# Attention with two MoE layers on one core: a weight's split parts kept in DRAM, two small scalings made one, and a path for probabilities turned by DMA

## The chip, the cores and the metric

The kernel runs on 1 core of one Trainium2 chip. The metric is the device time of one execution in microseconds (us), the median of several runs; less is better.

## The reference

Attention over 4 batches, 8 heads, 576 positions of 64 features, in which each row keeps its 32 largest scores; its output, as 2304 tokens of 512 features, goes through two feed-forward layers.

```python
scores = (q @ k.T) / 8
kth    = 32nd largest score of the row
scores = where(scores >= kth, scores, -1e9) - max
attn   = exp(scores) / (sum(exp(scores)) + 1e-9)
x = attn @ v                                    # [2304, 512]
x = (1 / (1 + exp(-(x @ w_gate))) * (x @ w_val)) @ w_out    # d_ff 1536
out = max(x @ w_in, 0)**2 @ w_out2                          # d_ff 2048
```

Weights arrive as float64, everything else as float32; the output is float32.

## The kernel before

**Tiles and chunks.** The 2304 tokens are 18 tiles of 128. They are worked through in 11 chunks: chunks 0 to 3 of one tile, chunks 4 to 10 of two. For each chunk all 8 heads go through attention, two heads at a time (class `Pair`, line 199), and then the chunk goes through the two layers. One tile of one head is called a unit here: 128 rows of scores, 144 units in all.

**A unit.** `scores` (line 262) multiplies the turned query by the head's keys on TensorE (PE); keys are split in two parts, kept in DRAM and loaded per head into one of three buffers `kst` (line 236). ScalarE (ACT) copies the scores to `S` (284). `softmax` (287) finds the 32nd largest of each row on VectorE (DVE) with four MAX8 and three MATCH_REPLACE8 passes (294, 300). GpSimd (POOL) makes two numbers a row of it, the mask's and the exponential's bias (304, 305, tile `bs`), ACT and POOL mask the scores (306, 307), ACT takes the exponential and its sum (308), DVE the reciprocal (312, 313), POOL scales the row (322). `transpose` (325) turns the probabilities on PE with matmuls against an identity (340, 358), ACT copies them back (341), and `values` (363) multiplies them by the values in float32 (373). In chunks 0 and 1 the scaling is done by the turning matmul (338).

**Weights.** 64-bit words are loaded 512 KB at a time into `wpool`, a pool of 35 slots, converted to float32, and from chunk 1 on used as two float16 parts: `split` (498) makes the high part on ACT (502) and the low part on DVE (505), every fourth time on POOL (507, 508). Of the 35 slots the split weights hold 34 for good once all are made; eight of these are of `w_out2`, called w2.

**The two layers.** Chunk 0 is computed in plain float32 (`moe32`, 740). The others run `moe` (614): each product is three float16 matmuls. Layer 1 is `l1_pair` (584) and `l1_acc` (620); then comes the turn (lines 660 to 675): ACT squares the result, PE sums columns (`x2pq`, 666), DVE takes the largest (`x2cm`, 668) and the scale `x2s` of it (124 to 129), and ACT and DVE write `x2` in two parts (672, 673). Layer 2 is `l2_pair` (689: `ph`, then `rh`) and `l2_acc` (712), which reads w2 from its eight tiles:

```python
acc2[:, i, 0:DM], gh[:, b_, ...], wblk("w2", a, f, 0, DM),   # lines 717 to 720
```

**Names.** The function begins with `NT, DM = out.shape` (line 87), so that within it, and in all that is defined in it, `DM` is 512.

**What sets the order.** The Tile scheduler orders each engine's instructions by priorities that the code gives: `at(t)` (963) for the weights and chunk 0, `attend` (951) for units, which are asked for a number of units ahead of each step of `moe`. All loads and stores are issued by SyncE (SP), one after the other, in the order that the scheduler sets.

## Time and profile before

| what | value |
|---|---|
| runs | 1314.05, 1313.09, 1314.70 us, median 1314.05 |
| the profiled execution: span from first to last instruction | 1312.3 us |
| what lies around that span, against the median | 1.75 us |
| PE busy | 1214.3 us (93%) |
| DVE busy | 1018.8 us (78%) |
| POOL busy | 838.6 us (64%) |
| ACT busy | 758.5 us (58%) |
| DMA | 113.00 MB, mean 86 GB/s |
| mean granted TensorE clock | 0.969 |

The profiled execution's own time isn't given apart from its span; the median of the runs stands 1.75 us above that span. An engine's busy share is a mean over stages, so the stage decides: the windows view gives busy time of each engine by stretch, the waits view what an engine stood still for, the timeline single instructions with the idle time before them in brackets and what ended it.

### The profile page before, as it was taken

What the parts mean: (1) busy time and instruction counts of PE and PEld (TensorE: products, weight loads), DVE (VectorE), ACT (ScalarE), POOL (GpSimd) and SP (SyncE); (2) the same over time, 40 slices, a digit from 0 to 9 for tenths busy, and PEclk for the clock granted to TensorE, in tenths of its full rate; (3) what the DMA queues carried; (4) which work ended last, traced back from release to release, by engine and by line L of the source; (5) the groups of instructions that cost most, each with busy time, mean ns of one, the idle gap of its engine ahead of it and who ended that gap; (6) DMA issues with size and microseconds to landing.
All of it is one profiled execution on the core that took longest, in us unless ns stands there. A gap on an engine that the chain in (4) does not pass through costs nothing.

```text
span 1312.3 us, 28283 instructions
## 1 busy us (share of the span) xinstructions
PE 1214.3 (93%) x10613; PEld 971.6 (74%) x10613; DVE 1018.8 (78%) x2192; ACT 758.5 (58%) x1500; POOL 838.6 (64%) x1124
## 2 busy tenths in 40 slices
PE   6746798989999899999999999999999999999998
PEld 4535686777978778777888678777876887787775
DVE  6999999999999999989899888985998698210010
ACT  4876767677666665666566655664566566323122
POOL 1988878888676675586567746674576557324223
PEclk9766899999999999999999999999999999999999
DMA  6967861221323221524211233321111110000000
GB/s 187 350 246 252 276 206 56 62 64 54 94 67 103 61 62 28 132 70 137 82 53 36 73 101 96 95 67 53 42 48 42 46 37 10 17 2 1 17 1 16
DMA packets 116328, 113.00 MB, mean 86 GB/s; under 512 B 73440, under 2 KB 87776, under 8 KB 116192
## 3 DMA queue, kind: packets, MB, share of 16 engines
q1 hardware_dynamic: 116192, 111.19, 28.3%
q8 instruction: 84, 1.38, 0.4%
q14 instruction: 52, 0.43, 0.1%
HBM read 96.99 MB, written 14.16 MB: 85 GB/s over the span
## 4 chain that ended last, share of the span: by engine, by line
PE 70%; DVE 14%; POOL 6%; ACT 3%; DMA 3%; issue 3%; SPq 1%; ACTq 0%; POOLq 0%; DVEq 0%
PE acc L717 13%; PE ph L696 12%; PE pg L593 9%; PE pv L593 9%; PE acc L633 9%; PE xp L373 6%; PE sp L281 6%; PE tp L340 4%; DVE mx L294 3%; DVE W L300 3%; POOL W L307 1%; PE qpt L244 1%; DMA wv_r<-in_moe_w_val_dram 1%; DVE wv_c L462 1%; POOL W L322 1%
## 5 line engine op out<-in xcount | busy, mean ns | idle before, releaser
L294 DVE MAX8 mx<-W 128x8 f32<-128x576 f32 x432 | 327.4, 758 | 7.7
L307 POOL TENSOR_TENSOR W<-S,W 128x576 f32<-128x576 f32 x144 | 208.1, 1445 | 32.6 <-ACT W L306 32.1
L696 PE MATMUL ph<-x,wi_w 128*128 128x256 f16 (+1 forms) x1920 | 209.2, 260 | 8.0 <-ACT x L672 7.4
L300 DVE MATCH_REPLACE8 W<-mx,W 128x576 f32<-128x576 f32 x288 | 213.7, 742 | 0.0
L717 PE MATMUL acc<-w_w,rh 128*128 128x512 f16 x816 | 195.8, 379 | 1.5 <-POOL rh L709 1.5
L696 PEld LDWEIGHTS <-wi_w 128*128 128x128 f16 x1920 | 167.2, 99 | 39.7 <-issue 10.4
L306 ACT ACTIVATE W<-S,bs 128x576 f32<-128x576 f32 x144 | 112.0, 778 | 108.2 <-POOL bs L304 107.9
L593 PE MATMUL pg<-xs,wg_w 128*128 128x256 f16 (+1 forms) x1440 | 156.0, 257 | 3.1 <-ACT xs L547 1.6
L308 ACT ACTIVATE W<-W,bs 128x576 f32<-128x576 f32 x144 | 112.0, 778 | 71.8 <-POOL W L307 71.3
L593 PE MATMUL pv<-xs,wv_w 128*128 128x256 f16 (+1 forms) x1440 | 152.7, 257 | 0.2 <-DVE x2cm L668 0.2
L281 PE MATMUL sp<-kst,qt 128*128 128x288 f32 x608 | 130.6, 327 | 9.0 <-ACT S L284 5.0
L593 PEld LDWEIGHTS <-wg_w 128*128 128x128 f16 x1440 | 122.4, 98 | 18.3 <-issue 2.7
L633 PEld LDWEIGHTS <-wo_w 128*128 128x128 f16 x1440 | 123.1, 98 | 16.6 <-issue 3.7
L593 PEld LDWEIGHTS <-wv_w 128*128 128x128 f16 x1440 | 122.7, 98 | 16.4 <-issue 3.3
L717 PEld LDWEIGHTS <-rh 128*128 128x128 f16 x816 | 77.7, 98 | 76.4 <-POOL rh L709 2.0
L605 DVE TENSOR_TENSOR th<-pv,th 128x512 f32<-128x512 f32 (+1 forms) x60 | 36.2, 603 | 119.1 <-PE pv L593 117.9
L633 PE MATMUL acc<-gh,wo_w 128*128 128x256 f16 (+1 forms) x1200 | 124.8, 254 | 2.4 <-POOL gh L609 2.4
L294 DVE MAX8 mx<-S 128x8 f32<-128x576 f32 x144 | 107.4, 746 | 15.7 <-ACT S L284 15.4
L708 POOL TENSOR_TENSOR r<-r 128x512 f32<-128x512 f32 (+1 forms) x80 | 74.7, 936 | 59.8 <-ACT rh L707 58.8
L341 ACT COPY PT<-tp 128x512 f32<-128x512 f32 x144 | 83.7, 581 | 47.6 <-PE tp L340 39.3
L322 POOL TENSOR_SCALAR we<-W,rz 128x64 f32<-128x64 f32 x128 | 41.5, 324 | 108.0 <-DVE rz L313 72.7
L300 DVE MATCH_REPLACE8 W<-mx,S 128x576 f32<-128x576 f32 x144 | 106.8, 742 | 0.3 <-issue 0.3
(297 smaller groups left out, 2224.8 us busy)
## 6 DMA issues: line engine op xcount, KB each, us to landing
kst<-ks SPq DMA_DIRECT2D x104, 288.0 KB, 2.9
v<-in_v_dram SPq DMA_DIRECT2D x112, 128.0 KB, 2.2
qn<-in_q_dram SPq DMA_DIRECT2D x128, 64.0 KB, 2.2
wi_r<-in_moe_w_in_dram SPq DMA_DIRECT2D x16, 512.0 KB, 6.8
w_r<-in_moe_w_out_dram SPq DMA_DIRECT2D x16, 512.0 KB, 4.7
wg_r<-in_moe_w_gate_dram SPq DMA_DIRECT2D x12, 512.0 KB, 8.0
wv_r<-in_moe_w_val_dram SPq DMA_DIRECT2D x12, 512.0 KB, 7.2
wo_r<-in_moe_w_out_dram SPq DMA_DIRECT2D x12, 512.0 KB, 7.0
```

Source lines behind the costliest of these rows:

```text
L281: nc.tensor.matmul(sp[:, e, 0:HALF], l, r, start=(x == 0), stop=(x == len(ops) - 1))
L294: m8 = nc.vector.max(mx[:, r], cur)
L300: nc.vector.match_replace(wk, mx[:, r], cur, NEG)
L306: nc.scalar.activation(wk, ss, AF.Relu, bias=bs[:, 0:1], scale=-BIG)
L307: nc.gpsimd.tensor_tensor(wk, ss, wk, op=ALU.subtract)
L308: nc.scalar.activation(wk, wk, AF.Exp, bias=bs[:, 1:2], scale=SCALE, accum_out=bs[:, 2:3])
L341: nc.scalar.copy(ptr[:, :, i * P : (i + 1) * P], tp.rearrange("p (c t) -> p c t", c=CB))
L373: nc.tensor.matmul(xp[j * D : (j + 1) * D, o : o + n], vj, pj, start=(si == 0 and c == 0), stop=(c == NB - 1), skip_group_check=True,)
L593: nc.tensor.matmul(pp[:, e * N : (e + 1) * N], wblk(wd, a, c, f0, P), xs[:, b_, c, :], start=(e == 0 and n == 0), stop=(n == 3 * KM - 1), ...
L633: nc.tensor.matmul(acc[:, d // 2, (d % 2) * N : (d % 2 + 1) * N], wblk("wo", a, f, d * P, P), gh[:, b_, e * N : (e + 1) * N], start=(f == ...
L696: nc.tensor.matmul(ph[:, e * N : (e + 1) * N], wblk("wi", a, c, f0, P), x2[:, b_, c, :], start=(e == 0 and n == 0), stop=(n == 3 * KM - 1) ...
L717: nc.tensor.matmul(acc2[:, i, 0:DM], gh[:, b_, e * N + i * P : e * N + (i + 1) * P], wblk("w2", a, f, 0, DM), start=(f == 0 and x == 0), s ...
```

## The change

1. **`bs`.** The two POOL operations of a unit on 128x1 (lines 304, 305) become one on 128x2, the first and the last of the row's 32 maxima times a constant tile `bsc` that two DVE memsets fill at the start.
2. **w2.** `split` writes each of w2's eight split tiles (512 KB) to DRAM (`w2s`). `l2_pair` of every chunk from 1 on loads the tile it needs into a slot of `wpool` (`w2t`), and `l2_acc` reads that. So w2 no longer holds eight slots.
3. **A second path for probabilities and values**, for chunk indices of `DM` and more: float16 parts of the scaled probabilities, turned by a DMA, and values in two float16 parts that are prepared once and loaded from DRAM; such units' `tail` comes two units later (`TLAG`) instead of one. The module gets a constant `DM = 4`; line 87, which sets `DM` in the function, stays.
4. `rz` gets a second operation, times 1.0 in chunk indices below `DM`.

The diff, cut to its core:

```diff
+DM = 4
+WE = 3
+TLAG = 2
+PSC = float(2.0**14)
...
+    bsc = const.tile([P, 2], F32, name="bsc")
+    nc.vector.memset(bsc[:, 0:1], -SCALE)
+    nc.vector.memset(bsc[:, 1:2], BIG)
...
+    def prep_values(b, hp):
+        vn = wpool.tile([P, 2 * CB + 1, D], F32, tag="w", name=f"vn_{b}_{hp}")
+        load_v(vn, b, hp)
...
+        d = dpool.tile([P, 2 * (2 * CB + 1) * D], F16, name=f"vs_{b}_{hp}", tag=f"vs_{b}_{hp}")
+        nc.sync.dma_start(d, v16.rearrange("p a c d -> p (a c d)"))
+        vscr[(b, hp)] = d
...
-            nc.gpsimd.tensor_scalar(bs[:, 0:1], mx[:, TOPK // 8 - 1, 7:8], BIG, None, op0=ALU.mult)
-            nc.gpsimd.tensor_scalar(bs[:, 1:2], mx[:, 0, 0:1], -SCALE, None, op0=ALU.mult)
+            nc.gpsimd.tensor_tensor(
+                bs[:, 0:2], mx.rearrange("p a b -> p (a b)")[:, 0 : TOPK : TOPK - 1], bsc, op=ALU.mult
+            )
...
-            nc.vector.tensor_scalar(rz, bs[:, 2:3], 1e-9, None, op0=ALU.add)
+            nc.vector.tensor_scalar(
+                rz, bs[:, 2:3], 1e-9, 1.0 if self.ci < DM else 1.0 / PSC, op0=ALU.add, op1=ALU.mult
+            )
...
-            return wk, ident
+            if self.ci < DM:
+                return wk, ident
+
+            wt = apool.tile([P, 2 * SM + 4 * ST], F16, tag="PT", bufs=2, name=f"w16_{tt}_{h}")
+            w16 = wt[:, 0 : 2 * SM].rearrange("p (a k) -> p a k", a=2)
+            nc.scalar.copy(w16[:, 0], wk[:, 0:SM])
+            nc.gpsimd.tensor_tensor(w16[:, 1], wk[:, 0:SM], w16[:, 0], op=ALU.subtract)
...
+            nc.sync.dma_start_transpose(
+                self.pt[j][:, :, i * P : (i + 1) * P], wt[:, 0 : 2 * SM]
+            )
...
         def transpose(self, j, i, wk, dg):
+            if self.ci >= DM:
+                return
...
+        if name == "w2":
+
+            d = dpool.tile([P, 2 * 2 * 512], F16, name=f"w2s_{pi}", tag=f"w2s_{pi}")
+            nc.sync.dma_start(d, t.rearrange("p a e f -> p (a e f)"))
+            w2scr[pi] = d
...
         def l2_pair(fp):
+            w2t[fp] = wpool.tile([P, 2, 2, 512], F16, tag="w", name=f"w2t_{ci}_{fp}")
+            nc.sync.dma_start(w2t[fp].rearrange("p a e f -> p (a e f)"), w2scr[fp])
...
-                            wblk("w2", a, f, 0, DM),
+                            w2t[fp][:, a, e, :],
...
-                if n > 0:
-                    tail(n - 1)
+                while lagging and n - lagging[0] >= (TLAG if units[lagging[0]][0].ci >= DM else 1):
+                    tail(lagging.pop(0))
```

How the change moves instructions, on three engines. Numbers at the end of a name tell buffers apart; `x2cm` and `x2pq` here are those of chunk 1.

DVE at chunk 1's turn, before: the largest of the columns, `x2cm`, and behind it three of the five low parts of w2 and of the second layer's other weight (`w_w`, `wi_w`); the other two stand further on.

```order
L294 MAX mx_0_3391<-S_0_3196 128x8
L668 TENSOR_REDUCE x2cm_3286<-x2pq_3279 128x1
L300 MATCH_REPLACE W_0_3390<-mx_0_3391,S_0_3196 128x576
L294 MAX mx_0_3391<-W_0_3390 128x8
...
L505 SCALAR_TENSOR_TENSOR w_w_2439<-w_c_1812,w2s,w_w_2439 128x1024
L505 SCALAR_TENSOR_TENSOR wi_w_2516<-wi_c_1624,wis,wi_w_2516 128x1024
L505 SCALAR_TENSOR_TENSOR wi_w_2519<-wi_c_1638,wis,wi_w_2519 128x1024
```

DVE at the same place, with the change: the last four of these low parts, and ahead of `x2cm` also a MATCH_REPLACE and a second MAX of the next unit.

```order
L613 SCALAR_TENSOR_TENSOR wi_w_2511<-wi_c_1615,wis,wi_w_2511 128x1024
L613 SCALAR_TENSOR_TENSOR wi_w_2514<-wi_c_1629,wis,wi_w_2514 128x1024
L613 SCALAR_TENSOR_TENSOR w_w_2530<-w_c_1827,w2s,w_w_2530 128x1024
L613 SCALAR_TENSOR_TENSOR w_w_2578<-w_c_1839,w2s,w_w_2578 128x1024
L344 MAX mx_0_3389<-S_0_3193 128x8
L350 MATCH_REPLACE W_0_3388<-mx_0_3389,S_0_3193 128x576
L344 MAX mx_0_3389<-W_0_3388 128x8
L780 TENSOR_REDUCE x2cm_3282<-x2pq_3275 128x1
```

All five low parts that stood behind `x2cm` now stand ahead of it, and so does that pair of passes.

PE from the turn of chunk 1 to the first product of its second layer (`ph_0`), before:

```order
L340 MATMUL tp_6_3204<-ident,W_6_3003 128x128 x4
L244 MATMUL qpt_1_3344<-ident,qn_1_3186 128x128 x2
L666 LDWEIGHTS ones
L666 MATMUL x2pq_3279<-x_1_3278,ones 128x128
L696 LDWEIGHTS wi_w_2030
L696 MATMUL ph_0_3304<-x_1_3278,wi_w_2030 128x128
```

and with the change:

```order
L331 MATMUL sp_1_3336<-kst_1_0_3191,qt_0_0_2975 128x288 x4
L423 MATMUL tp_6_3201<-ident,W_6_3001 128x128 x4
L294 MATMUL qpt_1_3342<-ident,qn_1_3183 128x128 x2
L778 LDWEIGHTS ones
L778 MATMUL x2pq_3275<-x_1_3274,ones 128x128
L331 MATMUL sp_2_3491<-kst_2_0_3333,qt_1_0_3345 128x288 x4
L812 LDWEIGHTS wi_w_2020
L812 MATMUL ph_0_3302<-x_1_3274,wi_w_2020 128x128
```

The scores `sp_2` have moved ahead of `ph_0`. Before `ph_2` the same is true of `tp_7`, `xp_3` and `sp_3`.

SP at that time with the change (before, the same queue holds the `kst` and `qn` loads without the rows of `w2s` and `w2t`):

```order
L620 DMA w2s_2581<-w_w_2578 128x2048
L805 DMA w2t_5_3660<-w2s_2521 128x2048
L286 DMA kst_4_0_3602<-ks_2_247 128x576
L262 DMA qn_3_3738<-in_q_dram 128x2x64 x2
L805 DMA w2t_6_3699<-w2s_2533 128x2048
L805 DMA w2t_7_3781<-w2s_2581 128x2048
L805 DMA w2t_0_4588<-w2s_2177 128x2048
L286 DMA kst_5_0_3746<-ks_2_247 128x576
```

The loads of w2's tiles stand between the loads of keys and queries, here those of chunk 2 already behind those of chunk 1; in chunks 4 to 8 all eight of a chunk stand close together.

## Rows read from the trace of the kernel before

**Rows 1.** Windows: engines' busy us (and instructions), granted clock, DMA share, GB/s, by stretch.

```profile
33.00:164.00 131.00, 83.65 (x553) 67.62 (x552) 129.55 (x221) 94.55 (x186) 116.12 (x93) 0.73 0.81 281
164.00:330.00 166.00, 147.24 (x1532) 122.50 (x1531) 157.56 (x298) 117.83 (x220) 139.35 (x156) 0.98 0.31 89
330.00:560.00 230.00, 220.27 (x2461) 186.00 (x2459) 218.19 (x512) 146.43 (x321) 149.80 (x259) 1.00 0.29 78
1115.00:1312.00 197.00, 189.61 (x1476) 144.22 (x1476) 20.46 (x49) 52.47 (x87) 66.55 (x69) 0.99 0.03 9
```

The columns after the stretch and its length are PE, PE's weight loads, DVE, ACT, POOL.

**Rows 2.** Waits of PE from 330 us on: total us, times, longest.

```profile
PE ph L696 <- ACT x L672: 4.1, 4, 1.9
PE sp L281 <- ACT S L284: 2.9, 2, 2.6
PE sp L281 <- DMA kst<-ks: 1.4, 1, 1.4
...
PE acc L633 <- POOL gh L609: 1.1, 3, 0.5
```

**Rows 3.** POOL's groups by form: busy us, mean ns of one, idle before.

```profile
L322 POOL TENSOR_SCALAR we<-W,rz 128x64 f32<-128x64 f32 x128 | 41.5, 324 | 108.0 <-DVE rz L313 72.7 <-ACT PT L341 6.4 <-ACT th L603 4.5
...
L305 POOL TENSOR_SCALAR bs<-mx 128x1 f32<-128x1 f32 x144 | 35.3, 245 | 36.6 <-DVE mx L294 28.6 <-DVE rz L313 1.3 <-DVE rz L312 1.3
L304 POOL TENSOR_SCALAR bs<-mx 128x1 f32<-128x1 f32 x144 | 33.0, 229 | 71.1 <-DVE mx L294 29.8 <-DVE rz L313 25.1 <-DVE x2s L126 4.1
```

**Rows 4.** Windows of line 305 alone, one instruction a unit.

```profile
330.00:1312.00 982.00, 23.97 (x115) 1.00 0.20 56
```

**Rows 5.** Timeline of DVE around chunk 1's turn: start, us, instruction, idle before.

```profile
289.99 0.29 DVE L668 TENSOR_REDUCE x2cm<-x2pq 128x1 f32<-128x128 f32 x1 [0.30 <-PE x2pq L666]
...
290.26 0.74 DVE L300 MATCH_REPLACE8 W<-mx,S 128x576 f32<-128x576 f32 x1
...
291.31 0.75 DVE L294 MAX8 mx<-W 128x8 f32<-128x576 f32 x1
...
295.69 1.27 DVE L505 SCALAR_TENSOR_TENSOR w_w<-w_c,w2s,w_w 128x1024 f16<-128x1024 f32 x1
...
298.33 1.26 DVE L505 SCALAR_TENSOR_TENSOR wi_w<-wi_c,wis,wi_w 128x1024 f16<-128x1024 f32 x1
...
301.04 2.04 DVE L505 SCALAR_TENSOR_TENSOR wi_w<-wi_c,wis,wi_w 128x1024 f16<-128x1024 f32 x1
...
311.75 1.28 DVE L505 SCALAR_TENSOR_TENSOR w_w<-w_c,w2s,w_w 128x1024 f16<-128x1024 f32 x1 [0.46 <-ACT w_w L502]
...
314.26 1.75 DVE L505 SCALAR_TENSOR_TENSOR w_w<-w_c,w2s,w_w 128x1024 f16<-128x1024 f32 x1
```

**Rows 6.** Windows, from chunk 1's turn to chunk 2's; columns as in rows 1.

```profile
290.00:366.00 76.00, 69.69 (x877) 59.45 (x877) 72.54 (x162) 51.92 (x112) 59.27 (x92) 0.96 0.26 72
```

**Rows 7.** Timeline of PE behind chunk 1's turn.

```profile
292.68 1.01 PE L696 MATMUL ph<-x,wi_w 128*128 128x128 f16 x8 [2.73 <-ACT x L672]
294.24 4.25 PE L696 MATMUL ph<-x,wi_w 128*128 128x128 f16 x40 [0.55 <-ACT x L672]
298.30 0.78 PE L281 MATMUL sp<-kst,qt 128*128 128x288 f32 x4
...
300.67 0.66 PE L340 MATMUL tp<-ident,W 128*128 128x128 f32 x4 [0.57 <-POOL W L322]
...
304.27 1.09 PE L373 MATMUL xp<-PT,v 128*64 128x128 f32 x16
```

**Rows 8.** DMA issues: KB each, median us from issue to landing.

```profile
w_r<-in_moe_w_out_dram SPq DMA_DIRECT2D x16, 512.0 KB, 4.7
wg_r<-in_moe_w_gate_dram SPq DMA_DIRECT2D x12, 512.0 KB, 8.0
```

**Rows 9.** Query loads `qn` from issue to landing, at 30 to 200 us and at 300 to 1000 us.

```profile
DMA to landing us min/median/max: 1.8/4.0/8.1
DMA to landing us min/median/max: 1.8/2.1/3.8
```

**Rows 10.** Windows of line 340 alone, PE's turning of probabilities; columns PE and weight loads.

```profile
330.00:1312.00 982.00, 73.63 (x468) 54.24 (x468) 1.00 0.20 56
```

More of the change, by code (lines that the diff above doesn't have):

```diff
@@ L174, in prep_keys, with load_v @@
             kscr[(b, 2 * hp + j)] = d[j].rearrange("a d s -> (a d) s")
+    vscr = {}
+    def load_v(t, b, hp):
+        src = v[b, 2 * hp : 2 * hp + 2]
+        for j in range(2):
+            nc.sync.dma_start(
+                t[:, j * CB : (j + 1) * CB], src[j, 0:SM].rearrange("(p c) d -> p c d", c=CB)
+            )
+            nc.sync.dma_start(t[j * ST : (j + 1) * ST, 2 * CB], src[j, SM:S])
+    def prep_values(b, hp):
+        vn = wpool.tile([P, 2 * CB + 1, D], F32, tag="w", name=f"vn_{b}_{hp}")
+        load_v(vn, b, hp)
+        v16 = wpool.tile([P, 2, 2 * CB + 1, D], F16, tag="w", name=f"v16_{b}_{hp}")
+        nq = mpool.tile([P, 2], F32, tag="vnq", name=f"vnq_{b}_{hp}")
+        nb = mpool.tile([P, 1], BF16, tag="vnb", name=f"vnb_{b}_{hp}")
+        nc.scalar.activation(v16[:, 1].bitcast(BF16), vn, AF.Square, accum_out=nq[:, 0:1])
+        pq = ps_t.tile([P, 512], F32, tag="tr", name=f"vpq_{b}_{hp}")
+        nc.scalar.copy(nb, nq[:, 0:1])
+        nc.tensor.matmul(pq[:, 0:1], ones, nb, start=True, stop=True)
+        nc.scalar.copy(nq[:, 1:2], pq[:, 0:1])
+        s, inv = pow2_scale(nq[:, 1:2], f"vs_{b}_{hp}", tag="vsc", bufs=2)
+        nc.gpsimd.tensor_scalar(
+            vinv[:, b, hp : hp + 1], inv, float(1.0 / PSC), 1.0, op0=ALU.mult, op1=ALU.mult
+        )
+        nc.scalar.activation(v16[:, 0], vn, AF.Copy, scale=s)
+        nc.vector.scalar_tensor_tensor(
+            v16[:, 1], vn, s, v16[:, 0], op0=ALU.mult, op1=ALU.subtract
+        )
+        d = dpool.tile([P, 2 * (2 * CB + 1) * D], F16, name=f"vs_{b}_{hp}", tag=f"vs_{b}_{hp}")
+        nc.sync.dma_start(d, v16.rearrange("p a c d -> p (a c d)"))
+        vscr[(b, hp)] = d
+    SPLIT = ((0, 0), (0, 1), (1, 0))
     def pieces(tt):
@@ L376, in values @@
                             pj,
-                            start=(si == 0 and c == 0),
-                            stop=(c == NB - 1),
+                            start=(si == 0 and x == 0),
+                            stop=(x == len(ops) - 1),
                             skip_group_check=True,
                         )
-            nc.scalar.copy(self.xt[:, self.hp, :], xp[:, 0 : self.N])
+            if self.ci < DM:
+                nc.scalar.copy(self.xt[:, self.hp, :], xp[:, 0 : self.N])
+                return
+            for b, o, n in self.segs:
+                nc.scalar.activation(
+                    self.xt[:, self.hp, o : o + n],
+                    xp[:, o : o + n],
+                    AF.Copy,
+                    scale=vinv[:, b, self.hp : self.hp + 1],
+                )
     REBIAS = float(2.0**-112)
@@ L488, in scale @@
         cx = const.tile([P, 1], F32, name=name + "cx")
-        dg = apool.tile([P, P], BF16, tag="we", bufs=3, name=f"{name}_d")
+        dg = apool.tile([P, P], BF16, tag="we", bufs=WE, name=f"{name}_d")
         nc.vector.tensor_tensor(dg, gram, ident, op=ALU.mult)
@@ L861, in attention @@
         work = {}
+        lagging = []
         def keys(pi):
@@ L880, in head @@
                 pr.queries(pr.tts[1:])
+                for tt in chunks[min(pr.ci + 1, nchunk - 1)] if pr.ci >= DM - 1 else ():
+                    for b, _, _, _ in pieces(tt):
+                        if (b, pr.hp) not in vscr:
+                            prep_values(b, pr.hp)
                 keys(pi + 1)
@@ L926, in attention @@
                 head(n + 1)
-                if n > 0:
-                    tail(n - 1)
+                while lagging and n - lagging[0] >= (TLAG if units[lagging[0]][0].ci >= DM else 1):
+                    tail(lagging.pop(0))
             work[n] = pr.softmax(j, i, ready.pop(n))
+            lagging.append(n)
             yield
-        tail(len(units) - 1)
+        while lagging:
+            tail(lagging.pop(0))
         yield
```

73 lines of the change are left out of this document (57 added, 16 removed).

## The prediction

> **What bounds the kernel now.** I read the windows first, then PE's waits, then the one place where the order moves. In the windows the reader is to see three stages [rows 1]. From 33 to 164 us DVE is busy 129.55 of 131 us: it converts weights and finds maxima, and it is the bound. From 164 to 330 us DVE still has 157.56 of 166 us, with POOL at 139.35 and PE at 147.24 not far behind; nothing is alone the bound, DVE is nearest. From 330 us on PE leads: 220.27 of 230 us to 560, and at the end, where attention is over, 189.61 of 197 us with DVE at 20.46. So a microsecond saved on POOL or DVE counts only before about 330 us, or where PE waits for it. The waits of PE after 330 us show how little that is [rows 2]: 4.1 us at the turns between the layers, 2.9 us for scores that ACT can't copy yet, 1.4 us once for a late key load, 1.1 us for POOL's part of a product. And work of PE that is pushed back behind 330 us stays in the time unless such a wait swallows it.
>
> **The change, part by part. The turned path isn't built.** The module says `DM = 4`, but the function's own `DM` is 512, and the chunk indices run to 10. So `ci < DM` always holds: no split probabilities, no turning DMA, no prepared values, `tail` one unit later as before, and `rz` times 1.0 in the same instruction. PE keeps its turning matmuls. This part costs and saves nothing. What is left are `bs`, w2, two memsets ahead of the first load's landing (nothing), and a new order.
>
> **`bs`.** Two POOL instructions of 245 and 229 ns a unit [rows 3] become one. The trace has no 128x2 form; its ends are the shorter of the two, 229 ns, and the 128x64 form, 324 ns, and I take 245, the nearest in size. That saves 229 ns a unit, 33 us of POOL's time over 144 units. The merged one waits for the last maximum, which the mask needs anyway, and nothing is queued behind it that went ahead before, so I exclude a loss. Of the 144 units 115 run after 330 us [rows 4], where POOL is not the bound: at most PE's 1.1 us for POOL come back [rows 2]. The other 29 save 6.6 us of POOL under DVE's bound; all of DVE's idle time there is 1.45 + 8.44 = 9.89 us [rows 1], and that idle time ends on many things. Ends: 0 and −9.9 us. I take −1.0: in the first stage DVE is 99% busy, so hardly anything can come of it, and in the second POOL is one of three engines.
>
> **The turn of chunk 1.** Five low parts and one pair of maximum passes that stood behind `x2cm` on DVE now stand ahead of it. By their rows [rows 5] they are 1.27 + 1.26 + 2.04 + 1.28 + 1.75 = 7.60 and 0.74 + 0.75 = 1.49 us, 9.09 together; the 0.30 and 0.46 us that DVE waited there fill up, so `x2cm` comes 8.3 us later. What waits for it is PE, whose second layer of chunk 1 then starts late. Against that stand three things. PE gets work ahead of it that it did later before: two scores at 0.78, a turning at 0.66, a value product at 1.09 [rows 7], 3.3 us. From there to chunk 2's turn PE was idle for 76 − 69.69 = 6.31 us [rows 6]; of this the turn's own 2.73 + 0.55 [rows 7] stay, 3.0 can be filled. That leaves 8.3 − 3.3 − 3.0 = 2.0 us at chunk 2's turn. And DVE's work is only moved, so attention isn't later from there on; the 2.9 us that PE then waits for scores [rows 2] can swallow what is left. Ends: 0, if they swallow it all, and +8.3, if PE's fillers and idle time don't fit. I take half of the 2.0, +1.0.
>
> **w2 through DRAM.** Eight writes and 80 loads of 512 KB, 46 MB on top of 113. A 512 KB transfer lands in 4.7 to 8.0 us [rows 8]. Who waits for it is `acc` of that chunk. A tile's slot comes free when the chunk before has used it, and from then to its next use lies most of a chunk: 16 units at (1115 − 330)/115 = 6.8 us [rows 1, 4], 109 us. That hides the loads. In chunk 1 the tiles go out and come back, 9.4 to 16 us by the same rows, under the late turn and the first products of layer 2; were the cover gone for one tile, 8.0 us once. The other price is what stands behind the loads in SP's queue: keys and queries. A chunk's eight tiles are 4.19 MB, at the 281 GB/s of the busiest stretch [rows 1] 14.9 us. Keys have three buffers, so a head's load is asked for one to two heads ahead, 13.6 to 27.2 us with two units a head. A burst of 14.9 us fits into most of that, not into all; where it doesn't, the nearest row is PE's one late key load, 1.4 us [rows 2]. Ends: 0, and one such wait in each of chunks 1 to 8, 11.2 us (a gain is excluded, as nothing is taken off the queue). I take +0.5, about a third of one wait.
>
> Small loads do come later among large ones: the query loads land in a median of 4.0 us while weights are loaded and in 2.1 us later [rows 9]. So beside weights 1.9 us are added to a load, well under the burst's 14.9. The Trainium skill, "DMA: Bandwidth & Descriptors", section "Queues, rings and completion order", says that on each DMA engine descriptors are consumed in ring order; by that alone a key load right behind a burst would wait for all of it. The rows agree in sign and show a far smaller delay, with a queue that was never loaded with eight at a time in attention; the rule's outcome is the second rival.
>
> **The sum.** The profiled span of 1312.3 us and the 1.75 us around it make the median of 1314.05. Then −1.0 − 0 + 1.0 + 0.5 gives 1314.5 us. A measurement of this kernel can tell about 0.2% from no change, 2.6 us.
>
> **The rivals.**
>
> *The late turn stays.* If PE's fillers merely take the place of work that PE would have had anyway while waiting, the lag at chunk 2's turn is 8.3 − 3.0 = 5.3 us, and from 330 us on PE has no room but the waits [rows 2]. For it: 96% and more of PE afterwards [rows 1]. Against it: the 2.9 us of waits for scores. It decides once more than 2.9 + 2.6 us of the 8.3 are still there after the fillers. About 1319.5 us; chance 0.17.
>
> *Keys behind the bursts.* The loads of a chunk stand close together in SP's queue, and a key load behind them is late by more than its lead, in half of chunks 1 to 8: 4 × 1.4 = 5.6 us, about 1320 us. For it: even now one key load is late [rows 2], without any such burst. Against it: DVE has a unit of scores in hand, and PE other work between. It decides where a burst exceeds 13.6 us, the shorter lead; at 281 GB/s it does by 1.3 us. Chance 0.18.
>
> *POOL was the bound of the second stage.* Then the 20 or so units there give back 229 ns each, and the splits on POOL too come earlier: 4 to 5 us, 1310 us. For it: PE's waits for POOL right behind chunk 1's turn, such as 0.57 us [rows 7], and 139.35 of 166 us on POOL. Against it: DVE's 157.56. Chance 0.20.
>
> *The path is built after all.* Then PE would lose the turning matmuls, 73.6 us after 330 us [rows 10], about 1240 us before what the value products add. The order speaks plainly against it: chance 0.01.
>
> **How the numbers follow.** No change has 0.44, and 1314.5 us is its time; the two slower rivals make 0.35, the faster ones 0.21. The range must reach to all three near rivals, as each holds nearly 0.2: from 1308, which is POOL's case with a little more of the 9.9 us, to 1322, the later keys with two stalls more than counted less what the waits swallow. What lies beyond, in both tails, is the 0.01, both slower rivals at once, and the far ends of the bounds.
>
> **What would show it.** POOL's time falls by 33 us, to about 806, with one 128x2 form of 144. PE's time stays within a few us of 1214, its turning matmuls are all there, and no DMA turns anything. DMA moves about 159 MB. In DVE's timeline `x2cm` of chunk 1 stands some 8 us later than at 290 us, and at chunk 2's turn PE is 2 us behind or less. If instead PE's waits show key loads in several chunks, the second rival holds; if `x2cm` comes no later and chunk 2's turn lies earlier than 366 us, the third. I am wrong in the mechanism if PE waits for w2's tiles themselves, or if the end moves though chunk 2's turn doesn't.

## The result, and the profile after

The changed kernel takes 1325.14 us (median of 4 runs, 1324.66 to 1326.33) beside 1314.38 us for the kernel before on the same chip: a ratio of 1.0083 [1.0065, 1.0101], slower by 10.8 us. The prediction was 1314.5 us, 1308 to 1322; the time lies above its range.

The page of the kernel after begins with the busy times, and its second part has the granted clock in 40 slices:

```profile
span 1322.8 us, 28281 instructions
...
PE 1227.5 (93%) x10613; PEld 982.2 (74%) x10613; DVE 1020.4 (77%) x2194; ACT 760.7 (58%) x1500; POOL 799.9 (60%) x980
...
PEclk9855989998999999999999999999999999999999
...
DMA packets 129000, 159.14 MB, mean 120 GB/s; under 512 B 74848, under 2 KB 89184, under 8 KB 128864
```

POOL lost 38.7 us (forecast 33) and DMA grew by 46 MB (as forecast). PE does the same matmuls, and its busy time grew by 13.2 us while its idle time shrank from 98.0 to 95.3 us. The loss doesn't look like one big wait. The windows say where it sits (stretch, length, PE, weight loads, DVE, ACT, POOL, granted clock, DMA share, GB/s):

```profile
33.00:164.00 131.00, 90.64 (x587) 74.27 (x587) 130.14 (x217) 92.46 (x183) 109.32 (x84) 0.73 0.80 276
164.00:330.00 166.00, 140.75 (x1394) 118.05 (x1393) 157.00 (x296) 115.82 (x214) 133.32 (x131) 0.93 0.49 152
330.00:560.00 230.00, 222.63 (x2509) 187.49 (x2507) 214.23 (x501) 147.29 (x323) 142.88 (x228) 1.00 0.35 102
...
1115.00:1322.00 207.00, 200.16 (x1548) 151.14 (x1545) 29.14 (x67) 57.42 (x97) 72.25 (x75) 0.99 0.13 49
```

Against [rows 1] the second stage is the one that changed: by 330 us PE has begun 1394 matmuls there instead of 1532, it was busy 6.5 us less, and its granted clock fell from 0.98 to 0.93. That drop takes 0.05 x 166 = 8.3 us of full clock from PE in this execution. It isn't 8.3 us of loss: the mean clock of the whole kernel, 0.969 in the profile before and 0.961 here, doesn't set the time. In the 56 executions of the kernel before beside e1 to e16 it lies between 0.957 and 0.967; the 26 at 0.961 or less have a median of 1313.99 us, the others 1313.71. A lower clock costs where PE is what the stage waits for. After 330 us PE is as busy as before, so what it has not done by then stands at the end: 1115 us to the end is 10 us longer.

The merged `bs` by form, against [rows 3]:

```profile
L354 POOL TENSOR_TENSOR bs<-mx,bsc 128x2 f32<-128x2 f32 x144 | 32.1, 223 | 75.7 <-DVE mx L344 52.5 <-DVE rz L366 16.8 <-DVE rz L363 6.4
```

The waits of PE from 330 us on, against [rows 2]:

```profile
PE sp L331 <- ACT S L334: 4.3, 3, 2.1
PE ph L812 <- ACT x L784: 2.5, 3, 1.6
...
PE acc L745 <- POOL gh L721: 0.7, 1, 0.7
```

No row of that view names w2's tiles or keys. So neither the loads of `w2t` nor key loads behind them cost the changed kernel a wait after 330 us. Chunk 1's turn is in PE's and DVE's timelines (start, us, instruction, idle before), against [rows 5, 7]; first PE:

```profile
285.51 2.29 PE L745 MATMUL acc<-gh,wo_w 128*128 128x128 f16 x20 [3.54 <-POOL gh L721]
...
294.99 0.22 PE L745 MATMUL acc<-gh,wo_w 128*128 128x128 f16 x1 [2.02 <-ACT gh L720]
296.65 2.61 PE L745 MATMUL acc<-gh,wo_w 128*128 128x128 f16 x23 [1.44 <-POOL gh L721]
...
303.42 0.79 PE L331 MATMUL sp<-kst,qt 128*128 128x288 f32 x4 [1.39 <-ACT S L334]
304.76 0.61 PE L812 MATMUL ph<-x,wi_w 128*128 128x128 f16 x8 [0.54 <-ACT x L784]
306.19 1.44 PE L812 MATMUL ph<-x,wi_w 128*128 128x128 f16 x12 [0.82 <-ACT x L784]
```

and DVE:

```profile
302.07 0.29 DVE L780 TENSOR_REDUCE x2cm<-x2pq 128x1 f32<-128x128 f32 x1 [1.11 <-PE x2pq L778]
```

The turn comes 12.1 us late, not 8.3, and DVE stood idle for 1.11 us ahead of `x2cm`. What came late is PE's column sum: layer 1 itself ends late, with 7.0 us of PE's waits for `gh` in the three rows above. The kernel before, from 164 to 330 us, has:

```profile
PE acc L633 <- POOL gh L609: 1.3, 3, 0.6
```

Who holds up `gh` is in POOL's timeline of the kernel after:

```profile
280.87 2.98 POOL L616 TENSOR_TENSOR w_w<-w_c,w_w 128x1024 f16<-128x1024 f32 x1
283.81 2.28 POOL L721 TENSOR_TENSOR gh<-th,gh 128x256 f16<-128x256 f32 x2
286.08 2.08 POOL L615 TENSOR_SCALAR w_c<-w_c,w2s 128x1024 f32<-128x1024 f32 x1
...
290.05 2.13 POOL L616 TENSOR_TENSOR w_w<-w_c,w_w 128x1024 f16<-128x1024 f32 x1
292.15 1.37 POOL L716 TENSOR_SCALAR th<-th 128x256 f32<-128x256 f32 x1
```

Splits made by POOL (L615, L616) stand between the steps of layer 1 (`th`, `gh`). They have moved ahead of the turn like DVE's low parts. Counted in the order of the traces, 16 high parts on ACT and four low parts on POOL stand ahead of `x2cm` with the change, ten and two before. POOL's steps also take longer beside DVE's low parts: `th` above starts while one runs (290.49 to 293.26 us) and takes 1.37 us; the `th` at 273.89 us, with none beside it, 0.40. Behind the turn ACT is no later than before: it writes `x2` at 304.23 us, 2.16 us behind `x2cm` in both kernels.

Two windows of the same profile show the clock at that place:

```profile
295.60:302.40 6.80, 5.38 (x37) 5.04 (x36) 5.25 (x14) 3.89 (x9) 3.54 (x6) 0.50 0.98 386
305.80:309.20 3.40, 3.01 (x24) 2.94 (x24) 3.33 (x9) 1.80 (x5) 2.18 (x3) 0.50 0.93 318
```

At 295 and 306 us PE runs at 0.50, its lower level of 1.2 GHz, right behind the waits above.

How the lag travels is read from the start of `x2cm` in each chunk (us; the change's lag in the last row):

| chunk | 1 | 2 | 3 | 4 | 5 | 6 | 7 | 8 | 9 | 10 |
|---|---|---|---|---|---|---|---|---|---|---|
| before | 290.0 | 366.1 | 443.8 | 548.7 | 695.5 | 828.1 | 952.9 | 1071.9 | 1179.8 | 1263.1 |
| after | 302.1 | 374.4 | 451.7 | 558.7 | 703.7 | 837.8 | 961.5 | 1081.2 | 1190.1 | 1273.3 |
| later by | 12.1 | 8.3 | 7.9 | 10.0 | 8.2 | 9.7 | 8.6 | 9.3 | 10.3 | 10.2 |

8.3 us are there at chunk 2's turn and never come back; some 2 us more gather later. So the question is what in the change makes the stretch around chunk 1's turn late.

### The profile page after: what moved, and what is told of

Read it like the earlier page. It is cut to its first block, busy times and chain, and to the rows that moved or that the text cites. A ratio compares the mean times of both kernels' runs of the same rounds, so it can differ in the third digit from the quotient of the medians.

```text
span 1322.8 us, 28281 instructions
## 1 busy us (share of the span) xinstructions
PE 1227.5 (93%) x10613; PEld 982.2 (74%) x10613; DVE 1020.4 (77%) x2194; ACT 760.7 (58%) x1500; POOL 799.9 (60%) x980
## 4 chain that ended last, share of the span: by engine, by line
PE 70%; DVE 6%; POOL 4%; ACT 3%; issue 2%; DMA 1%; SPq 0%; ACTq 0%; DVEq 0%; POOLq 0%
PE ph L812 14%; PE acc L833 13%; PE acc L745 9%; PE pg L705 9%; PE pv L705 8%; PE xp L471 6%; PE sp L331 5%; PE tp L423 4%; DVE mx L344 2%; DVE W L350 2%; POOL W L358 1%; PE qpt L294 1%; DVE wo_w L613 1%; ACT W L357 1%; POOL we L375 1%
## 5 line engine op out<-in xcount | busy, mean ns | idle before, releaser
L833 PE MATMUL acc<-w2t,rh 128*128 128x512 f16 x816 | 195.2, 379 | 0.0
L331 PE MATMUL sp<-kst,qt 128*128 128x288 f32 x608 | 133.5, 332 | 9.8 <-ACT S L334 8.6
L375 POOL TENSOR_SCALAR we<-W,rz 128x64 f32<-128x64 f32 x128 | 45.4, 355 | 131.2 <-DVE rz L366 85.6
```

The costliest lines, as they stand in the source:

```text
L331: nc.tensor.matmul(sp[:, e, 0:HALF], l, r, start=(x == 0), stop=(x == len(ops) - 1))
L833: nc.tensor.matmul(acc2[:, i, 0:DM], gh[:, b_, e * N + i * P : e * N + (i + 1) * P], w2t[fp][:, a, e, :], start=(f == 0 and x == 0), stop= ...
```

## The experiments

Times are medians in us. The kernel before took 1313.54 (e1 to e4), 1313.39 (e5 to e8), 1314.28 (e9 to e12), 1313.84 (e13 to e16) and 1313.15 (e17, e18) on the same chip; each ratio is against that. "Turn 1" and "turn 2" are the starts of `x2cm` in chunks 1 and 2 (before: 290.0 and 366.1).

| run | time | ratio, 95% interval | turn 1 | turn 2 |
|---|---|---|---|---|
| e1 only `bs` merged | 1324.07 | 1.0080 [1.0065, 1.0094] | 292.3 | 371.9 |
| e2 only w2 through DRAM | 1319.15 | 1.0044 [1.0030, 1.0058] | 297.7 | 372.3 |
| e3 change, chunk 1 reads w2 on chip | 1323.13 | 1.0069 [1.0054, 1.0084] | 292.5 | 372.1 |
| e4 change, last low parts behind the turn | 1317.54 | 1.0027 [1.0016, 1.0038] | 294.0 | 366.9 |
| e5 e1, scores behind `ph_0` | 1321.03 | 1.0058 [1.0045, 1.0070] | 291.6 | 370.0 |
| e6 e4, scores behind `ph_0` | 1319.07 | 1.0039 [1.0025, 1.0053] | 294.4 | 367.4 |
| e7 e1, the wait filled | 1323.08 | 1.0075 [1.0062, 1.0088] | 291.5 | 371.4 |
| e8 change, second path really built | 1341.30 | 1.0203 [1.0187, 1.0219] | 304.0 | 382.4 |
| e9 `bs` merged from chunk 4 on | 1318.38 | 1.0030 [1.0020, 1.0041] | 290.2 | 366.3 |
| e10 before, turn behind two splits | 1322.69 | 1.0063 [1.0048, 1.0078] | 289.8 | 373.7 |
| e11 e1, last low parts behind the turn | 1331.31 | 1.0131 [1.0114, 1.0147] | 291.9 | 375.8 |
| e12 e2, last low parts behind the turn | 1322.82 | 1.0070 [1.0055, 1.0085] | 291.8 | 365.7 |
| e13 `bs` merged, order of before | 1311.80 | 0.9990 [0.9981, 0.9999] | 288.5 | 365.4 |
| e14 before, order of e1 | 1326.96 | 1.0106 [1.0091, 1.0120] | 292.1 | 372.9 |
| e15 change, PE, DVE, POOL in order of before | 1326.28 | 1.0098 [1.0084, 1.0111] | 288.4 | 368.4 |
| e16 e14, turns filled | 1324.46 | 1.0083 [1.0070, 1.0096] | 291.6 | 372.4 |
| e17 order of before, chunk 1 reads w2 on chip | 1319.67 | 1.0049 [1.0035, 1.0063] | 288.1 | 364.1 |
| e18 e17, keys ahead of one burst | 1312.58 | 0.9993 [0.9981, 1.0005] | 288.1 | 365.1 |

### Which part of the change: e1 to e4

e1 is the change with w2 kept on chip (from the change):

```diff
-        if name == "w2":
...
-            nc.sync.dma_start(d, t.rearrange("p a e f -> p (a e f)"))
...
-            w2t[fp] = wpool.tile([P, 2, 2, 512], F16, tag="w", name=f"w2t_{ci}_{fp}")
...
-                            w2t[fp][:, a, e, :],
+                            wblk("w2", a, f, 0, DM),
```

> The change without w2 in DRAM: only the merged bs operation (and the two memsets and rz's second operation). Five low parts stand behind chunk 1's x2cm on DVE again, as before. Theory A (the late turn of chunk 1 makes the loss): x2cm near 290 us, time 1313 to 1315 us. Theory B (traffic of w2's 46 MB makes it): the same time, so this run does not part A from B. Theory C (the merged POOL operation, or the new order that comes with it, makes the loss): about 1324 us.

e2 is the reverse: those lines put into the kernel before, all else as it was.

> The kernel before with w2 through DRAM and nothing else; bs stays in two operations. All low parts stand ahead of chunk 1's x2cm. A and B: 1322 to 1327 us, x2cm of chunk 1 at 300 to 304 us under A. C: 1314 us.

e3 leaves only chunk 1's eight loads out (72 stay):

```diff
+            if ci > 1:
+                w2t[fp] = wpool.tile([P, 2, 2, 512], F16, tag="w", name=f"w2t_{ci}_{fp}")
...
+                            (w2t[fp][:, a, e, :] if ci > 1 else wblk("w2", a, f, 0, DM)),
```

> The change, but chunk 1 reads w2 from the tiles that split made; w2 is still written to DRAM, and chunks 2 to 10 load it (72 of the 80 loads). Five low parts stand behind x2cm again. A: x2cm near 290 us, time 1313 to 1316 us. B: at least nine tenths of the loss stay, about 1324 us.

e4 makes the last seven splits behind the turn, by their place in the program and an ordering edge, which fixes the scheduler's order and adds no wait on a semaphore:

```diff
+            if turned:
+                tc.add_manual_dep(lo.ins, turned[0].name, NOSYNC, reason="behind the turn")
...
+                    while len(todo) > LATE and todo[0][0] <= n:
```

> The change with all 80 loads, but the last seven splits (five low parts on DVE) are made only behind chunk 1's turn. A: x2cm near 290 us; the loads of w2 for chunk 1 are then short of time, as the split, the write and the load follow each other, so PE may wait for w2t there for some us; time 1314 to 1320 us. B: about 1325 us with x2cm near 290 us.

Measured: either part alone costs (+10.5 and +5.6 us), together 10.8, so their costs don't add. e2 missed all its theories: it lies between them. In e1 no low part has moved ahead of `x2cm`, the turn is 2.3 us late, and yet e1 is as slow as the whole change. That sinks the theory that the late `x2cm` alone is the cause. e1 moves no byte of w2, so the traffic isn't needed for the loss either; e3, without chunk 1's loads, has e1's late turn and about e1's loss. e4 leaves 4.0 of the 10.8 us, with the turn 4.0 us late instead of 12.1. Up to 280 us its order is that of the change on every engine, and the 16 high parts on ACT and four low parts on POOL still stand ahead of `x2cm`. So of the changed kernel's loss 8.1 us at the turn, and about 6.8 us of the time, go with DVE's five low parts. What e1 has in PE's timeline is a new wait, longer than the 2.73 us of [rows 7], in front of the scores of a later unit that now stand ahead of `ph_0`:

```profile
297.20 1.33 PE L331 MATMUL sp<-kst,qt 128*128 128x288 f32 x4 [5.21 <-ACT S L334]
298.33 1.08 PE L805 MATMUL ph<-x,wi_w 128*128 128x128 f16 x8
```

### Is it that wait: e5 to e7

e5 is e1 with an edge that keeps these scores behind `ph_0`; e6 is e4 with the same edge:

```diff
+                    if (tt, h) in EDGE and first_ph:
+                        tc.add_manual_dep(mm.ins, first_ph[0].name, NOSYNC, reason="ph first")
```

> The run with bs alone showed PE standing 5.21 us at chunk 1's turn for ACT's copy of scores, with the first product of layer 2 (ph_0) behind those scores in its order, and half the granted clock for 10 us from there. Here one ordering edge more on PE: those scores (head 2 of tile 3) go behind the first pair of products of chunk 1's layer 2; nothing else is changed. Theory D (the loss is PE's order there: scores ahead of ph_0 that can't run yet): the wait ahead of ph_0 falls to about 3 us, chunk 2's x2cm comes at 366 to 369 us against 371.9 us, and the time is 1316 to 1320 us against 1324. Theory C (the merged POOL operation itself is late in each unit): 1323 to 1325 us.

> All 80 loads of w2, the last seven splits behind chunk 1's turn, and the same edge for the scores of head 2 of tile 3. Theories A and D together: what is left of the loss (3 to 4 us in the run with the low parts late) shrinks by the 1.8 us that PE stood for those scores and by the slower clock behind it: 1313.5 to 1316.5 us. Theory B (the loads themselves cost): 1317 us or more.

e7 is e1 with 56 products of a constant in the wait, whose results nothing reads: extra work, to hold the clock.

```diff
+            for _ in range(56 if ci == 1 else 0):
+                nc.tensor.matmul(
+                    pq[:, 256:384], ones, ones, start=True, stop=True, skip_group_check=True
+                )
```

> The run with bs alone, and 56 more products of constants (128x128, bfloat16) on PE, whose results nothing uses, between chunk 1's column sums and the scores that wait there; they lie inside the 5.21 us in which PE stood still. Theory E (most of the loss is not the wait but the half clock that follows it, and PE's being busy keeps the clock): no half clock from 296 to 306 us, PE's busy time falls though it does more, and the time is 1319 to 1322 us. If the wait alone counts: 1324 to 1325 us, and the clock there may be full all the same.

Measured: e5 is 3.0 us below e1, e7 1.0 us (their ranges overlap, so hardly told apart), e6 1.5 us above e4 (they overlap too). None came out where theory D or E had put it. The scheduler is free in all three and chooses another order behind chunk 1's turn, so these times aren't the price of the edit alone. With the scores out of the way PE waits just as long for the turn itself:

```profile
296.90 1.01 PE L809 MATMUL ph<-x,wi_w 128*128 128x128 f16 x8 [5.58 <-ACT x L783]
...
298.97 1.44 PE L809 MATMUL ph<-x,wi_w 128*128 128x128 f16 x12 [1.05 <-ACT x L783]
```

So in e1 and e5 the scores are only the first to hit it; what is late is ACT, which writes both `S` and `x2`.

### The path that isn't built: e8

The module's constant gets a name of its own, so that chunks 4 to 10 take the path of split, DMA-turned probabilities:

```diff
-DM = 4
+CD = 4
...
-            if self.ci < DM:
+            if self.ci < CD:
```

> The change with its module constant under a name of its own, so that chunks 4 to 10 take the path with split probabilities turned by DMA and values in two float16 parts. By rows of before PE loses 448 turning matmuls and 56 of the ends, about 85 us, and its value products in float32 become three in float16 each; POOL gains a subtraction of 128x512 in each of 112 units, at 1.16 us as in the split of layer 2 some 130 us, ACT a copy of 0.58 us, 65 us. If PE stays the bound and POOL's 511 of 785 us in the attention stage take it: 1240 to 1290 us. Rival: the turning DMAs, or POOL, become the bound of the attention stage: over 1324 us.

Measured: 1341.30 us, against the 1240 that the prediction's last rival gave. PE's busy time does fall, to 1183.4 us, but from 560 to 1115 us it is then idle for 49 us. Its waits after 330 us:

```profile
PE sp L331 <- ACT S L334: 22.1, 7, 7.3
PE xp L471 <- DMA PT<-w: 14.0, 13, 3.2
PE ph L812 <- ACT x L784: 5.8, 4, 2.8
PE acc L833 <- DMA w2t<-w2s: 4.5, 6, 1.4
```

The rival priced what PE would save and none of what it would then wait for; the rival of the run's own expectation, over 1324 us, came true, though the largest wait is for ACT's copies of scores, which it didn't name.

### Order or operations, first attempts: e9 to e12

e9 merges `bs` in chunks 4 to 10 only, so that the stages up to chunk 2's turn keep their order:

```diff
+            if self.ci < 4:
...
+            else:
+                lo, hi = 1, 0
+                nc.gpsimd.tensor_tensor(
```

> The kernel before with the merged bs operation in chunks 4 to 10 alone, 112 of the 144 units; the order of all engines up to there, chunk 1's turn included, is that of before. Theory D2 (the loss with bs alone is the order that the scheduler then chose in the first 300 us, above all at chunk 1's turn, where steps of the turn on DVE and ACT stand behind weight splits; the operation costs nothing): 1311 to 1315 us, x2cm of chunk 1 at 290 us. Theory C (each merged operation comes late in its unit): 112/144 of the loss, about 1321 us.

e10 is the kernel before with two edges: at chunk 1's turn, `x2s` behind one more low part on DVE, and the high part of `x2` behind two more high parts of splits on ACT.

```diff
+            if ci == 1:
+                tc.add_manual_dep(p2[0], low[NLOW].name, NOSYNC, reason="low part first")
...
+                if ci == 1 and h == 0:
+                    tc.add_manual_dep(hi.ins, lohi[NLOW + 1].name, NOSYNC, reason="high part first")
```

> The kernel before, its bs in two operations and its w2 on chip, with two ordering edges alone: at chunk 1's turn the scale on DVE goes behind one more low part, and x2's high part on ACT behind two more high parts of splits, about as the run with bs alone had it. D2: x2cm stays at 290 us, ph_0 starts 3 to 7 us later than 292.7 us, half the granted clock lasts longer than 6.8 us there, chunk 2's x2cm comes at 369 to 373 us, and 1316 to 1322 us. If PE's later work swallows it, or if what counts is something else of the change: 1313 to 1315 us.

e11 and e12 give e1 and e2 the late low parts of e4 (the same lines).

> The run with bs alone, but the last seven splits stand behind chunk 1's turn on DVE, so that its scale and its two parts have nothing of the splits ahead of them there. D2: ph_0 within 4 us of x2cm, chunk 2's x2cm at 366 to 369 us, and 1315 to 1319 us against 1324; what is left of the loss lies ahead of the turn (x2cm 2.3 us late) and at the turns of chunks 3 and 4. C: 1323 to 1325 us.

> The run with w2 through DRAM alone (bs in two operations), but the last seven splits behind chunk 1's turn. Its loss of 5.6 us came with an x2cm of chunk 1 that was 7.7 us late. D2: x2cm at 290 to 293 us, and 1313 to 1316 us: the 80 loads and 8 writes cost nothing. B (the loads cost): 1318 to 1320 us.

Measured: e10 costs 8.4 us with no operation of the change in it. `x2cm` is on time, and behind it PE stands still:

```profile
295.96 1.33 PE L284 MATMUL sp<-kst,qt 128*128 128x288 f32 x4 [6.16 <-ACT S L287]
299.54 1.01 PE L709 MATMUL ph<-x,wi_w 128*128 128x128 f16 x8 [2.25 <-ACT x L683]
```

8.41 us of waits where [rows 7] had 3.28, and half clock from 294.0 to 307.6 us where before it was 291.3 to 298.2. That is 5.1 us more standing still and 6.7 us more at half clock, worth half of that; 8.5 in all, and chunk 2's turn is 7.6 us late. The two edges also let the scheduler choose another order on every engine from there to some 820 us, but the lag grows by only 1 us behind chunk 2's turn. e9 missed both of its theories: it is on time at turn 2 and still loses 4.1 us, 3.4 of the 4.4 us of lag in `x2cm` behind 828 us. From 379 us on its order is another one: the merging reorders later stages too. e11 and e12 both missed. In e11 the late low parts hold up layer 2, and PE waits for `r` and `x` (chunk 2's turn 9.8 us late). In e12 PE waits for w2's own tiles, which their late splits send out late:

```profile
302.37 0.38 PE L732 MATMUL acc<-w2t,rh 128*128 128x512 f16 x1 [1.61 <-DMA w2t<-w2s]
...
306.67 1.46 PE L732 MATMUL acc<-w2t,rh 128*128 128x512 f16 x6 [1.23 <-DMA w2t<-w2s]
```

But these waits aren't what e12 loses: its turn 2 is on time, and `x2cm` is 3.7 us late in chunk 4 and 8.7 in chunk 5. Which part of its later order does that wasn't followed. So placing low parts by hand is no cure; these edges made other orders too. What tells order and operations apart is to hold the whole order and change the operations alone.

### Order or operations, told apart: e13 to e16

In e13 `bs` is merged in all 144 units, and edges between neighbours force the instructions of each of the five engines into the order of before. e14 is the reverse: the operations of before, forced into e1's order.

```diff
+    for seq in _orders():
+        for a, b_ in zip(seq, seq[1:]):
+            tc.add_manual_dep(ins[b_], ins[a].name, NOSYNC, reason="order of before")
```

> The run with bs alone (merged operation in all 144 units), with ordering edges that put every instruction of PE, DVE, ACT, POOL and SP in the order that the kernel before has. Theory G (the loss is the scheduler's order alone, the merged operation costs nothing): 1311 to 1315 us, x2cm of chunk 1 at 289 to 291 us and of chunk 9 near 1179.8 us. Theory C (the merged operation itself, waiting for the last maximum, holds up each unit): 1318 us or more, with the lag growing evenly over the attention stage.

> The other way round: the kernel before, bs in two operations, with every instruction of the five engines in the order that the run with bs alone had. G: 1321 to 1327 us, with the longer turn of chunk 1 (PE waiting about 5 us for scores) and half clock there. C: 1313 to 1316 us.

Measured: e13 1311.80 us, e14 1326.96. Against before, with the two operations of `bs` the other order costs 13.1 us (e14), and with the merged one 10.5 (e1) where the old order gives back 2.0 (e13). So the order costs about 13 us with either, and the merged operation saves 2 to 3 us in either (e13's own interval is 0.1 to 2.5 us). In the traces e13 has the order of before on every engine, and e14 that of e1. No run forces the kernel before into its own order; but if the edges cost something themselves, they raise e13 and e14 alike, and by the two savings, 2.0 and 2.6 us, that would be 0.3 us. The two in the window from 290 to 305 us (columns as in rows 1; e13's turn is at 288.5 us, e14's at 292.1), e13:

```profile
290.00:305.00 15.00, 11.47 (x132) 10.16 (x132) 14.93 (x30) 11.27 (x22) 10.06 (x12) 0.78 0.13 34
```

e14:

```profile
290.00:305.00 15.00, 8.49 (x66) 7.36 (x64) 14.78 (x35) 10.73 (x19) 11.54 (x13) 0.66 0.19 50
```

DVE, ACT and POOL are as busy in both; PE gets through half the matmuls. Why is in the timelines of DVE and ACT. In the kernel before DVE's `x2s`, the scale, comes at 291.98 us, 2.0 behind `x2cm`, and ACT writes the high part of `x2` at once:

```profile
292.15 0.47 ACT L672 ACTIVATE x<-acc,x2s 128x256 f16<-128x256 f32 x1 [0.93 <-DVE x2s L126]
```

In e14 a low part stands on DVE between `x2cm` and the scale:

```profile
292.09 0.28 DVE L669 TENSOR_REDUCE x2cm<-x2pq 128x1 f32<-128x128 f32 x1
...
293.01 1.27 DVE L506 SCALAR_TENSOR_TENSOR w_w<-w_c,w2s,w_w 128x1024 f16<-128x1024 f32 x1
...
294.93 0.14 DVE L127 TENSOR_SCALAR x2s<-x2s_1n 128x1 int32<-128x1 int32 x1
```

and on ACT two more high parts than before stand ahead of `x2` (12 instead of 10). The second of them waits for DVE itself, and an exponential and a copy of scores follow:

```profile
294.32 1.15 ACT L503 ACTIVATE wi_w<-wi_c,wis 128x1024 f16<-128x1024 f32 x1 [1.12 <-DVE w_w L506]
295.58 0.78 ACT L309 ACTIVATE W<-W,bs 128x576 f32<-128x576 f32 x1
...
296.36 0.62 ACT L285 COPY S<-sp 128x576 f32<-128x576 f32 x1
296.88 0.48 ACT L673 ACTIVATE x<-acc,x2s 128x256 f16<-128x256 f32 x1
```

`x2cm` comes 2.1 us later than before, the scale 2.95, `x2` 4.73. At chunk 2's turn e14 is 6.8 us late, about half of its 13.1. The two halves have each been seen alone: e10 with chunk 1's turn reordered is 7.6 us late there, and e9, in which only the later order differs, ends 4.1 us late.

e15 is the whole change with PE, DVE and POOL held to the order of before (ACT and SP are free); e16 is e14 with 32 constant products, read by nothing, at the turns of chunks 1, 3 and 4.

> The whole change (merged bs, eight writes and 80 loads of w2), with PE, DVE and POOL in the order of the kernel before; ACT and SP in an order that the scheduler chose under it. G and loads that cost nothing: 1312 to 1317 us. B (the loads cost by themselves): 1317 us or more, with PE's waits on w2t or on keys to show for it.

> The kernel before in the order of the run with bs alone, as the run above, and at the turns of chunks 1, 3 and 4 another 32 products of constants (128x128) on PE, whose results nothing uses, behind the column sums, where PE waits. Everything else stands in the same order. Theory E (half the clock after a wait is a cost of its own, and PE's being busy averts it): the half-clock stretches near 450 and 556 us are gone and the one at 296 us is shorter, and the time is 3 to 6 us below that of the run above. If the clock only goes with the wait and costs little: within 1.5 us of it.

Measured: e16 is 2.5 us faster than e14 (1322.46 to 1324.87 against 1326.26 to 1328.15 us) though PE does more; expected were 3 to 6. The row from 561 to 568 us, e14:

```profile
561.00:568.00 7.00, 5.98 (x29) 4.75 (x29) 6.90 (x17) 4.21 (x9) 2.81 (x5) 0.51 0.80 221
```

e16:

```profile
561.00:568.00 7.00, 5.24 (x44) 4.28 (x45) 6.90 (x17) 4.27 (x9) 2.82 (x5) 1.00 0.93 243
```

So 2.5 us of the loss hang on PE's standing idle at these places, and in this row the clock is full where e14's is half. e15 came out on the side of theory B: with PE, DVE and POOL in the old order the change is as slow as in its own, for other reasons. ACT, whose order is free and another than before's, lets PE wait 4.0 us for `x` at chunk 1's turn. PE waits 3.2 us for w2's tiles in chunk 1, and once for keys, with half clock behind it:

```profile
848.65 1.33 PE L332 MATMUL sp<-kst,qt 128*128 128x288 f32 x4 [5.41 <-DMA kst<-ks]
```

### The old order with w2's loads: e17 and e18

e17 holds all five engines to the order of before and lets chunk 1 read w2 on chip, as in e3; e18 also issues chunk 6's eight `w2t` loads behind the key loads that PE waited for, the other engines unchanged.

> The change, but chunk 1 reads w2 from the tiles that split made (72 loads, for chunks 2 to 10), and all five engines in the order of the kernel before; on SP the writes and loads of w2 stand between the rows of that order where the scheduler put them. Against the run with the whole change in the old order PE's 3.2 us for w2t in chunk 1 are gone; the eight loads of chunk 6 still stand ahead of the key loads for head 5 of chunk 8, for which PE waited 5.4 us there. Theory H (in the old order the loads cost by two places, chunk 1's round trip and that key load, with the half clock behind them): x2cm of chunk 2 at 365 to 367 us, the wait for keys near 840 us still there, 1316 to 1321 us. If the loads cost nothing by themselves: 1311 to 1314 us. If they cost in another way: 1323 us or more.

> As the run above, and the eight loads of w2 for chunk 6 stand behind those key loads in SP's order; PE, DVE, ACT and POOL have the very same order. H: the wait for keys near 840 us falls to the 1.5 us of before or less, and the time is 4 to 7 us below the run above, 1311 to 1315 us; chunk 6's own w2t may then come late by a few us in its stead. If the key load's lateness is not the burst's doing: the same time as above.

Measured: 1319.67 and 1312.58 us. e17 is ahead of before until 828 us (`x2cm` 0.8 us early in chunk 6) and behind it in chunk 7 (4.6 late); between them lie one wait of 4.90 us for keys and 6.8 us at half clock (839.2 to 846.0). Its DMA issues from 820 to 850 us (KB each, median us to landing):

```profile
w2t<-w2s SPq DMA_DIRECT2D x7, 512.0 KB, 6.5
...
ks<-kp SPq DMA_DIRECT2D x2, 144.0 KB, 7.9
ks<-kn SPq DMA_DIRECT2D x2, 144.0 KB, 6.3
```

The same of e18:

```profile
ks<-kp SPq DMA_DIRECT2D x2, 144.0 KB, 2.5
ks<-kn SPq DMA_DIRECT2D x2, 144.0 KB, 2.5
```

In SP's queue stand the burst, writes of a later head's keys (`ks`), and then the key load that PE needs. Right behind the burst a write of 144 KB lands after 7.9 us instead of 2.5, and SP issues the key load at 838.89 us instead of 833.20. So what the burst costs is the load's late issue, not its landing: e17's key loads there land after 3.0 to 4.2 us, and e18's, which now have the burst behind them, after 5.8 to 6.2. PE's wait for keys falls to 2.3 us (1.4 before), not quite to what was expected. The Trainium skill, "DMA: Bandwidth & Descriptors", section "Queues, rings and completion order", the rule of ring order that the prediction weighed, agrees with the writes (7.9 and 6.3 us beside the burst's 6.5); for the key loads, issued well behind the burst in e17, no such delay shows (3.0 to 4.2 us). With the keys first, e18 stands 0.6 us below before where e13 stood 2.0: what w2 through DRAM costs in chunks 2 to 10 can't be told from nothing.

## Why the prediction was wrong

**"`bs` −1.0 us."** Right as the price of an operation: 223 ns (I took 245), and in the old order the merging gives 2.0 us (e13). Wrong in that I excluded a loss for it. The merged operation, with nothing else, makes the scheduler put two more splits, an exponential and a copy ahead of `x2` on ACT, and a low part between `x2cm` and its scale; that order, with all that goes with it, costs 10.5 us in e1 and 13.1 in e14. In the whole change the order is yet another: there `x2` follows `x2cm` as quickly as before, and the loss comes ahead of the turn.

**"`x2cm` 8.3 us late."** 12.1 us, and by another way. I took DVE's queue for the path: nine us of passes more, so `x2cm` later by that. But DVE waits 1.11 us for the column sum; the path is PE's layer 1, which waits 3.54, 2.02 and 1.44 us for `gh`. `gh` comes from ACT, DVE and POOL, and splits moved ahead on all three. I read the new order on DVE, PE and SP and left out ACT's six high parts and POOL's two low parts. The five low parts themselves took 1.52 + 2.08 + 1.59 + 1.33 + 2.77 = 9.29 us there, not 7.60. That e4 gives 8.1 us for them, close to my 8.3, is an agreement of sizes and not of the path; the other 4.0 us had no term.

**"Less 3.3 us of fillers, less 3.0 us of idle time."** From 12.1 the lag falls to 8.3 us at chunk 2's turn: 3.8 us, where I took off 6.3. The window from turn to turn, after:

```profile
302.00:374.00 72.00, 68.12 (x876) 58.66 (x876) 64.26 (x156) 46.10 (x107) 47.66 (x80) 0.97 0.52 162
```

PE does as many products between the turns as before (876 and 877 [rows 6]). So the fillers take nothing out of that stretch; they are the work that fills its idle time, and the sum took them off a second time. The idle time is 72 − 68.12 = 3.88 us against 6.31: 2.4 us were filled of the 3.0. The rest of the 3.8 is PE's busy time, at a clock of 0.97 against 0.96. And `sp_2` ahead of `ph_0`, which I took for a filler, itself waits for ACT (1.39 us after, 5.21 in e1).

**"Later waits swallow half."** They swallow nothing. PE's wait for scores grew from 2.9 to 4.3 us, and the 8.3 us at chunk 2's turn have become 10.2 at chunk 10's. This is the first rival, "the late turn stays", with its mechanism: the fillers merely take the place of other work. It was sized 5.3, where 8.3 and more came, as it too set out from 8.3 instead of 12.1.

**"w2 through DRAM +0.5 us."** Right as the price of transfers, if chunk 1 is left out and keys go first (e18); wrong as part of the change. Alone it costs 5.6 us (e2), in another order, with 7.1 us of PE's waits for `gh` and none for w2's tiles. That the freed slots bring that order about is likely, but no run shows it. The second rival, keys behind the bursts, didn't happen in the changed kernel. In e15 and e17 it did, as one wait of about 5 us rather than four of 1.4. The third, POOL as the bound, gave 4 to 5 us: the merging brings 2 to 3 in a fixed order, and e13's first turn is 1.5 us early.

What stays open: how the 4.0 us of the late turn that e4 leaves divide between ACT's high parts, POOL's low parts and the rest of the order, and what of the 2 us after chunk 2's turn is order and what clock. The whole change with all 80 loads was never run with all five engines in the old order: e15 leaves ACT and SP free, e17 and e18 leave chunk 1's loads out. The fastest kernel tried is e13; its gain, 0.1%, is below the 0.2% that the prediction took as the least that can be told.

## What to carry to other kernels

Where a scheduler sets the order, a change of a duration or a slot can also be a change of order, and with `bs` the order was worth some 13 us while the operation was worth 2 to 3. Compare the new order on every engine that feeds the bound one, not only on the engine that looks busiest, ask which of them ends the wait at a stage's turn, and price the waits with the clock behind them. Work that fills a wait and the wait that it fills are one term, not two. To learn what an edit itself is worth, hold the old order with edges and run both orders; and where bulk loads are added to a queue, look at the small writes and loads behind them.
